# Ten Q-projection units row-tiled in pairs, with the filler matmuls placed ahead of them

## Chip, cores, metric

One core of one Trainium2 chip. The metric is the device time of one execution in microseconds (us), median of several runs.

## The reference

Input x has 2048 rows (tokens) and D = 576 columns. Both branches read the same layer norm of x, and the output is x plus both.

```python
xn = layernorm(x)
q, k, v = heads(xn @ wqkv)                 # 32 heads of 18
phi = lambda t: where(t > 0, t + 1, exp(t)) + 1e-6
kv  = einsum("bhsd,bhse->bhde", phi(k), v);  z = phi(k).sum(tokens)
A   = (phi(q) @ kv) / (phi(q) . z + 1e-6) @ wo
B   = (gelu(xn @ w_gate) * (xn @ w_up)) @ w_down      # 576 -> 4608 -> 576
return x + A + B
```

## The kernel before

Everything is written in one fixed order per engine. In the profiles PE is TensorE and SP is SyncE. PSUM is one tensor of eight banks, and the code names the bank of each product. The Q projection is made in 20 units (4 token chunks of 512, 5 head chunks of 126 or 72 columns). A unit contracts 576 = 4 x 128 + 64 rows, so its fifth matmul uses half of the array. Each unit's result then passes phi on ScalarE (ACT), VectorE (DVE) and, for two of three units, POOL; every third is finished on VectorE by a two-input add. Between the units stand other matmuls, the "filler".

```python
def phi_tiles():
    e = awork.tile([P, D], F32, name="phi_e", tag="phi_e", bufs=3)
    a = awork.tile([P, D], F32, name="phi_a", tag="phi_a", bufs=2)

def q_unit(i):
    ...
    for kt in range(KT):                                   # 5 matmuls on the full array
        nc.tensor.matmul(ps, lhsT=wqkv_sb[:, kt, q0:q0 + rows], rhs=xnT[:, kt, cs], ...)
    e, a = phi_tiles()
    if i % 3 != 2:
        nc.scalar.activation(out=e, in_=ps, func=ACT.Relu, scale=-1.0)
        nc.vector.tensor_scalar(out=a, in0=ps, ...)        # reads the bank too
        nc.scalar.activation(out=e, in_=e, func=ACT.Exp, scale=-1.0)
        nc.gpsimd.tensor_tensor(out=pqT[...], in0=e, in1=a, op=ALU.add)
    else:
        nc.scalar.activation(out=e, in_=ps, func=ACT.Exp)
        nc.vector.tensor_scalar(out=a, in0=ps, ...)
        nc.vector.scalar_tensor_tensor(out=pqT[...], in0=e, in1=a, ...)   # two SBUF inputs

for i in range(2, NSC * NCH):                              # cut: copies, early Gram, z
    q_unit(i)
    if 5 <= i < 13:  ...two g_accumulate(n, G_B)           # 4 Gram matmuls per unit
    if 13 <= i < 13 + NCH:  den_mm(0, i - 13, q_banks.next())
    if i == 17:  kv_stage()

class _Unit:                       # gate/up: gate and up share the array, 64 rows each
    def p1(self):                  # lower half adds into bank 0, upper half into bank 1
        for kt in (4, 0, 1, 2, 3):
            self.mm(0, LO, kt, kt == 4, False); last = self.mm(1, HI, kt, kt == 4, False)
        self.turn = nc.sync.nop()  # waits for `last`
    def p2(self):                  # the halves change banks; the first waits for turn
        for kt in range(4):
            self.mm(1, LO, kt, ...); self.mm(0, HI, kt, ...)
# a gate/up block: load, p1(u0), load, p1(u1), p2(u0), gelu, p2(u1), gelu
```

## Time and profile before

| | before |
|---|---|
| time, median of the first 3 runs | 532.59 us (532.07 to 533.60) |
| profiled span | 530.5 us |
| PE busy | 522.6 us |
| first Q matmul to first gate/up matmul | 45.06 to 77.59, 32.53 us |

All later intervals start at the first Q matmul, because the start of the kernel scatters by up to 0.45 us from trace to trace (the first Q matmul is between 45.06 and 45.51).

### The profile page before, as it was taken

What the parts mean: (1) busy time and instruction counts of PE and PEld (TensorE: products, weight loads), DVE (VectorE), ACT (ScalarE), POOL (GpSimd) and SP (SyncE); (2) the same over time, 40 slices, a digit from 0 to 9 for tenths busy, and PEclk for the clock granted to TensorE, in tenths of its full rate; (3) what the DMA queues carried; (4) which work ended last, traced back from release to release, by engine and by line L of the source; (5) the groups of instructions that cost most, each with busy time, mean ns of one, the idle gap of its engine ahead of it and who ended that gap; (6) DMA issues with size and microseconds to landing.
All of it is one profiled execution on the core that took longest, in us unless ns stands there. A gap on an engine that the chain in (4) does not pass through costs nothing.

```text
span 530.5 us, 10752 instructions
## 1 busy us (share of the span) xinstructions
PE 522.6 (99%) x4532; PEld 314.3 (59%) x4532; DVE 248.7 (47%) x408; ACT 152.5 (29%) x288; POOL 70.3 (13%) x83
## 2 busy tenths in 40 slices
PE   7999999999999999999999999999999999999997
PEld 5887666444467754444477744444677544445775
DVE  7885666783338613333368233333485143333101
ACT  6887783323330003323200022323100132322000
POOL 4666542110002100000012000000021000000000
PEclk9999999999999999999999999999999999999999
DMA  8910006898510025555400055555100345540000
GB/s 283 248 30 1 1 2 184 261 270 267 143 39 12 23 78 153 148 150 157 135 12 12 12 153 162 146 157 153 49 22 13 94 143 158 155 135 1 12 12 22
DMA packets 98810, 55.85 MB, mean 105 GB/s; under 512 B 5322, under 2 KB 98378, under 8 KB 98762
## 3 DMA queue, kind: packets, MB, share of 16 engines
q1 hardware_dynamic: 98762, 55.17, 36.2%
q8 instruction: 35, 0.57, 0.4%
q14 instruction: 13, 0.11, 0.1%
HBM read 52.79 MB, written 2.36 MB: 104 GB/s over the span
## 4 chain that ended last, share of the span: by engine, by line
PE 95%; SPq 2%; DVE 1%; ACT 1%; issue 0%; DMA 0%
PE ps_all L505 51%; PE ps_all L576 27%; PE ps_all L310 4%; PE ps_all L581 4%; PE ps_all L280 4%; PE ps_all L238 3%; PE ps_all L227 1%; SPq L166 1%; PE ps_all L370 1%; SPq L168 0%; SPq L169 0%; DMA x_sb<-in_A_x_dram 0%; ACT xnT L230 0%; DVE xn L217 0%; PE ps_all L358 0%
## 5 line engine op out<-in xcount | busy, mean ns | idle before, releaser
L505 PE MATMUL ps_all<-xnT,wg 64*128 64x512 bf16 x1152 | 274.1, 377 | 0.0
L505 PE MATMUL ps_all<-xnT,wu 64*128 64x512 bf16 x1152 | 272.6, 377 | 0.9 <-SPq L514 0.3
L549 DVE TENSOR_TENSOR hT<-ps_all,gl 128x512 bf16<-128x512 f32 x144 | 99.6, 692 | 168.9 <-ACT gl L548 168.7
L548 ACT ACTIVATE gl<-ps_all 128x512 f32<-128x512 f32 x144 | 86.0, 597 | 316.7 <-PE ps_all L505 294.9
L505 PEld LDWEIGHTS <-wu 64*128 64x128 bf16 x1152 | 106.9, 94 | 70.9 <-SPq L514 8.7
L505 PEld LDWEIGHTS <-wg 64*128 64x128 bf16 x1152 | 107.0, 94 | 66.7 <-issue 0.3
L576 PE MATMUL ps_all<-wd_sb,hT 128*128 128x288 bf16 x1152 | 146.6, 286 | 0.0
L576 PEld LDWEIGHTS <-hT 128*128 128x128 bf16 x1152 | 112.2, 98 | 31.5 <-issue 1.9
L384 DVE RECIPROCAL den_sb<-den_sb 126x128 f32<-126x128 f32 (+1 forms) x80 | 68.3, 911 | 0.5
L385 POOL TENSOR_TENSOR pqT<-pqT,den_sb 126x512 bf16<-126x512 bf16 (+3 forms) x25 | 24.1, 965 | 301.5 <-DVE den_sb L384 298.2
L584 DVE TENSOR_TENSOR res<-ps_all,x_sb 128x288 bf16<-128x288 f32 x32 | 14.6, 458 | 88.3 <-PE ps_all L581 88.3
L505 PE MATMUL ps_all<-xnT,wr 64*128 64x512 bf16 x288 | 55.9, 377 | 0.0
L581 PE MATMUL ps_all<-m_sb,pqT 126*128 126x288 bf16 (+1 forms) x160 | 24.9, 286 | 0.0
L505 PEld LDWEIGHTS <-wr 64*128 64x128 bf16 x288 | 14.6, 94 | 17.4 <-issue 1.1
L310 PE MATMUL ps_all<-xnT,wqkv_sb 128*126 128x512 bf16 (+1 forms) x100 | 24.4, 380 | 0.0
L265 POOL TENSOR_TENSOR hT<-phi_e,phi_a 128x576 bf16<-128x576 f32 x16 | 22.5, 1404 | 8.9 <-ACT phi_e L264 4.9
L280 PE MATMUL ps_all<-hT,xn 128*128 128x288 bf16 (+3 forms) x192 | 23.6, 266 | 0.0
L238 PE MATMUL ps_all<-wqkv_sb,xnT 128*128 128x288 bf16 x160 | 22.4, 286 | 0.8 <-DVE xnT L230 0.6
L280 PEld LDWEIGHTS <-xn 128*128 128x128 bf16 (+1 forms) x192 | 18.2, 101 | 4.5
L320 POOL TENSOR_TENSOR pqT<-phi_e,phi_a 126x512 bf16<-126x512 f32 (+1 forms) x14 | 17.7, 1268 | 15.5 <-DVE phi_a L318 11.8
L581 PEld LDWEIGHTS <-pqT 126*128 126x128 bf16 (+1 forms) x160 | 15.5, 97 | 4.1
L238 PEld LDWEIGHTS <-xnT 128*128 128x128 bf16 x160 | 15.0, 98 | 4.5 <-DVE xnT L230 0.8
(58 smaller groups left out, 200.6 us busy)
## 6 DMA issues: line engine op xcount, KB each, us to landing
wg<-in_B_w_gate_dram SPq DMA_DIRECT2D x72, 256.0 KB, 2.9
wu<-in_B_w_up_dram SPq DMA_DIRECT2D x72, 256.0 KB, 3.4
wd_sb<-in_B_w_down_dram SPq DMA_DIRECT2D x12, 432.0 KB, 4.5
wr<-in_B_w_gate_dram SPq DMA_DIRECT2D x72, 32.0 KB, 2.7
wr<-in_B_w_up_dram SPq DMA_DIRECT2D x72, 32.0 KB, 3.1
out_dram<-res SPq DMA_DIRECT2D x15, 144.0 KB, 1.8
x_sb<-in_A_x_dram SPq DMA_DIRECT2D x3, 576.0 KB, 6.6
wqkv_sb<-in_A_wqkv_dram SPq DMA_DIRECT2D x2, 576.0 KB, 9.2
```

The costliest lines, as they stand in the source:

```text
L238: nc.tensor.matmul(ps_all[:, k_bank(n, hf), :HALF], lhsT=xnT[:, kt, n * P:(n + 1) * P], rhs=wqkv_sb[:, kt, D + hf * HALF:D + (hf + 1) * HALF],
L265: nc.gpsimd.tensor_tensor(out=pk[:, n, :], in0=e[:], in1=a[:], op=ALU.add)
L280: nc.tensor.matmul(ps_all[:m, b, col:col + w], lhsT=xn[:, n, j0:j0 + m], rhs=pk[:, n, d0:d0 + w], start=(n == 0 and col == 0), stop=(n == ...
L310: nc.tensor.matmul(ps, lhsT=wqkv_sb[:, kt, q0:q0 + rows], rhs=xnT[:, kt, cs], start=(kt == 0), stop=(kt == KT - 1),)
L320: nc.gpsimd.tensor_tensor(out=pqT[:rows, c, cs], in0=e, in1=a, op=ALU.add)
L384: nc.vector.reciprocal(out=d[:, h:h + P], in_=d[:, h:h + P])
L385: nc.gpsimd.tensor_tensor(out=pqT[:rows, c, cols], in0=pqT[:rows, c, cols], in1=d, op=ALU.mult)
L505: return nc.tensor.matmul(self.outs[i], lhsT=self.lhs(i, rows, kt), rhs=self.rhs(i, rows, kt), start=start, stop=stop, skip_group_check=True,)
L548: nc.scalar.activation(out=gl[:], in_=ps_all[:, b[0], :], func=ACT.Gelu_apprx_tanh)
L549: nc.vector.tensor_tensor(out=hT[:, GUB * k + i, :], in0=ps_all[:, b[1], :], in1=gl[:], op=ALU.mult)
L576: nc.tensor.matmul(acc, lhsT=hT[:, f, j * P:(j + 1) * P], rhs=wd_sb[:, f, hs], start=(f == 0), stop=False,)
L581: nc.tensor.matmul(acc, lhsT=pqT[:rows, c, ts_], rhs=m_sb[:rows, c, hs], start=False, stop=(c == NCH - 1),)
```

## The change

Two Q units of the second half share the array as two row tiles of 64 rows: 9 slots of two half matmuls in place of 10 matmuls. All filler is placed ahead, so that the ten units run without a switch between the array's two modes, next to gate/up, which is row-tiled already. Gate/up's ring of banks now starts at bank 1, and the ring of the later m_stage is shifted too. Core of the diff:

```diff
+    wq_lo = apool.tile([P, D], BF16, name="wq_lo")        # last 64 rows of Wq for the upper half
+        if which == 0:
+            nc.sync.dma_start(wq_lo[HP:P, :], A_wqkv[512:576, c])
+    banks = _Ring([1, 2, 3, 4, 5, 6, 7, 0])
-    for i in range(2, NSC * NCH):
+    for i in range(2, 2 * NCH):
...
+        if i >= 4:
+            for n in G_B_AT[i]:
+                g_accumulate(n, G_B)
+    for c in range(NCH):
+        den_mm(0, c, q_banks.next())
+    kv_stage()
+    q_banks = _Ring([7, 0, 1, 2, 3, 4, 5, 6])
+    for k, items in enumerate([[(2, 0), (2, 1)], [(2, 2), (2, 3)], [(2, 4), (3, 4)], [(3, 0), (3, 1)], [(3, 2), (3, 3)], None]):
+        if items:
+            u = q_pair(items)
+            u.p1()
+        if prev:
+            prev[1].p2()
+            for i, (sc, c) in enumerate(prev[0]):
+                q_phi(2 * k + i, sc, c, prev[1].outs[i])
+        prev = (items, u)
```

I number the paired units by the index that q_phi gets, 2 to 11; 2, 5, 8 and 11 are finished on VectorE. Unit 11 has bank 0.

More of the change, by code (lines that the diff above doesn't have):

```diff
@@ L283, in g_accumulate @@
                 )
+    G_B_AT = {4: (), 5: (0, 1), 6: (2, 3, 4), 7: (5, 6, 7), 8: (8, 9, 10, 11), 9: (12, 13, 14, 15)}
     vcopy, acopy = nc.vector.tensor_copy, nc.scalar.copy
@@ L298, with __init__, mm, p1 @@
     q_next = [0]
+    LO, HI = slice(0, HP), slice(HP, P)
+    SYNC = mybir.DependencyInfo(mybir.DependencyClass.Sync, mybir.DependencyReason.DATA)
+    banks = _Ring([1, 2, 3, 4, 5, 6, 7, 0])
+    class _Unit:
+        def __init__(self, outs, lhs, rhs):
+            self.outs, self.lhs, self.rhs = outs, lhs, rhs
+        def mm(self, i, rows, kt, start, stop):
+            return nc.tensor.matmul(
+                self.outs[i], lhsT=self.lhs(i, rows, kt), rhs=self.rhs(i, rows, kt),
+                start=start, stop=stop, skip_group_check=True,
+            )
+        def p1(self):
+            for kt in (4, 0, 1, 2, 3):
+                self.mm(0, LO, kt, kt == 4, False)
+                last = self.mm(1, HI, kt, kt == 4, False)
+            self.turn = nc.sync.nop()
+            tc.add_manual_dep(self.turn.ins, last.ins.name, SYNC, reason="the row tiles take turns on a bank")
+        def p2(self):
+            for kt in range(4):
+                m = self.mm(1, LO, kt, False, kt == 3)
+                if kt == 0:
+                    tc.add_manual_dep(m.ins, self.turn.ins.name, SYNC, reason="the bank's other row tile has written")
+                self.mm(0, HI, kt, False, kt == 3)
     q_banks = _Ring([7])
@@ L306, in q_unit @@
         q0 = DH * HOFF[c]
-        cs = slice(sc * SC, (sc + 1) * SC)
         ps = ps_all[:rows, q_banks.next(), :]
@@ L310, in q_unit, with q_pair, lhs, q_phi @@
             nc.tensor.matmul(
-                ps, lhsT=wqkv_sb[:, kt, q0:q0 + rows], rhs=xnT[:, kt, cs],
+                ps, lhsT=wqkv_sb[:, kt, q0:q0 + rows], rhs=xnT[:, kt, sc * SC:(sc + 1) * SC],
                 start=(kt == 0), stop=(kt == KT - 1),
             )
+        q_phi(i, sc, c, ps)
+    def q_pair(items):
+        rows = DH * HCH[items[0][1]]
+        b = [q_banks.next(), q_banks.next()]
+        outs = [ps_all[:rows, b_, :] for b_ in b]
+        def lhs(i, r, kt):
+            q0 = DH * HOFF[items[i][1]]
+            if kt == 4 and r.start:
+                return wq_lo[r, q0:q0 + rows]
+            return wqkv_sb[r, kt, q0:q0 + rows]
+        return _Unit(outs, lhs, lambda i, r, kt: xnT[r, kt, items[i][0] * SC:(items[i][0] + 1) * SC])
+    def q_phi(i, sc, c, ps):
+        rows = DH * HCH[c]
+        cs = slice(sc * SC, (sc + 1) * SC)
         e, a = phi_tiles()
@@ L464 @@
             g_copy(kt, pieces, part, copy)
-        if i == 10:
+        if i >= 4:
+            for n in G_B_AT[i]:
+                g_accumulate(n, G_B)
+        if i == 8:
             z_stage()
-        if 5 <= i < 13:
-            for n in (2 * (i - 5), 2 * (i - 5) + 1):
-                g_accumulate(n, G_B)
-        if 13 <= i < 13 + NCH:
-            den_mm(0, i - 13, q_banks.next())
-        if i == 17:
-            kv_stage()
+    for kt, pieces, part, copy in G_COPIES[14]:
+        g_copy(kt, pieces, part, copy)
+    for c in range(NCH):
+        den_mm(0, c, q_banks.next())
+    kv_stage()
+    q_banks = _Ring([7, 0, 1, 2, 3, 4, 5, 6])
+    prev = None
+    for k, items in enumerate([[(2, 0), (2, 1)], [(2, 2), (2, 3)], [(2, 4), (3, 4)], [(3, 0), (3, 1)], [(3, 2), (3, 3)], None]):
[7 more added lines that the diff above has]
+        prev = (items, u)
     den_jobs = [(0, c, q, 2) for c in range(NCH) for q in range(2)]
@@ L488, in load_wd_slice @@
             wd_loaded[0] += WDS
-    LO, HI = slice(0, HP), slice(HP, P)
-    SYNC = mybir.DependencyInfo(mybir.DependencyClass.Sync, mybir.DependencyReason.DATA)
-    banks = _Ring(list(range(8)))
-    class _Unit:
-        def __init__(self, outs, lhs, rhs):
-            self.outs, self.lhs, self.rhs = outs, lhs, rhs
-        def mm(self, i, rows, kt, start, stop):
-            return nc.tensor.matmul(
-                self.outs[i], lhsT=self.lhs(i, rows, kt), rhs=self.rhs(i, rows, kt),
-                start=start, stop=stop, skip_group_check=True,
-            )
-        def p1(self):
-            for kt in (4, 0, 1, 2, 3):
-                self.mm(0, LO, kt, kt == 4, False)
-                last = self.mm(1, HI, kt, kt == 4, False)
-            self.turn = nc.sync.nop()
-            tc.add_manual_dep(self.turn.ins, last.ins.name, SYNC, reason="the row tiles take turns on a bank")
-        def p2(self):
-            for kt in range(4):
-                m = self.mm(1, LO, kt, False, kt == 3)
-                if kt == 0:
-                    tc.add_manual_dep(m.ins, self.turn.ins.name, SYNC, reason="the bank's other row tile has written")
-                self.mm(0, HI, kt, False, kt == 3)
     def gu_pair(sc, k):
@@ L549, in gu_pair @@
             nc.vector.tensor_tensor(out=hT[:, GUB * k + i, :], in0=ps_all[:, b[1], :], in1=gl[:], op=ALU.mult)
-    m_banks = _Ring(list(range(2, 8)))
+    m_banks = _Ring([3, 4, 5, 6, 7, 0])
     def m_stage(chunks):
```

## The prediction

> **What bounds the kernel now.** I read the page first, then the chain of work that ended last, then the busy table by stage, then the timeline of the one stage that the change touches. The chain's sum by engine:
>
> ```profile
> PE 95%; SPq 2%; DVE 1%; ACT 1%; issue 0%; DMA 0%
> ```
>
> So a microsecond counts only if TensorE (PE) gives it up or is made to wait. The stages, cut at the points where the chain changes its kind of matmul (columns: stretch, length, busy time of PE, weight loads, VectorE, ScalarE, POOL, then clock, DMA share, GB/s):
>
> ```profile
> 0.00:45.00 45.00, 41.63 (x395) 34.21 (x396) 35.98 (x99) 36.12 (x85) 25.75 (x42) 1.00 0.59 165
> 45.00:77.60 32.60, 32.60 (x212) 22.03 (x211) 20.27 (x36) 24.53 (x47) 17.99 (x14) 1.00 0.00 1
> 77.60:149.00 71.40, 71.33 (x654) 34.74 (x654) 42.95 (x60) 24.51 (x42) 9.21 (x12) 1.00 0.74 216
> ```
>
> The second line is the Q stage: PE busy in all 32.60 us, no transfers, full clock. The third is the first quarter of gate/up, in row tiles already. Inside the Q stage:
>
> ```profile
> 65.63 0.60 ACT L323 ACTIVATE phi_e<-ps_all 126x512 f32<-126x512 f32 x1 [0.52 <-PE ps_all L310]
> 66.33 0.69 DVE L324 TENSOR_SCALAR phi_a<-ps_all 126x512 f32<-126x512 f32 x1 [0.43 <-ACT phi_e L323]
> 67.06 0.69 DVE L325 SCALAR_TENSOR_TENSOR pqT<-phi_e,phi_a 126x512 bf16<-126x512 f32 x1
> 67.26 0.60 ACT L317 ACTIVATE phi_e<-ps_all 126x512 f32<-126x512 f32 x1 [1.03 <-PE ps_all L310]
> 67.49 1.24 PE L310 MATMUL ps_all<-xnT,wqkv_sb 128*126 128x512 bf16 x5
> 67.96 0.69 DVE L318 TENSOR_SCALAR phi_a<-ps_all 126x512 f32<-126x512 f32 x1 [0.21 <-ACT phi_e L317]
> 68.57 0.38 PE L370 MATMUL ps_all<-pqT,zrep 126*126 126x512 bf16 x1
> 68.79 1.24 PE L310 MATMUL ps_all<-xnT,wqkv_sb 128*72 128x512 bf16 x5
> 68.80 1.27 POOL L320 TENSOR_TENSOR pqT<-phi_e,phi_a 126x512 bf16<-126x512 f32 x1 [2.21 <-DVE phi_a L318]
> ...
> 75.31 2.35 PE L310 MATMUL ps_all<-xnT,wqkv_sb 128*126 128x512 bf16 x10
> ...
> 77.59 0.39 PE L505 MATMUL ps_all<-xnT,wr 64*128 64x512 bf16 x2
> ...
> 78.12 1.27 DVE L318 TENSOR_SCALAR phi_a<-ps_all 126x512 f32<-126x512 f32 x2
> ```
>
> PE starts are what to read, since a matmul's 0.38 us overlaps the next. 67.49 to 68.57 is a unit of five matmuls: 1.08 us, 0.2166 each. 68.57 to 68.79 is one denominator matmul, 0.22. No gap between them. The other engines wait for PE here (0.5 to 2.2 us in brackets), because filler stands between Q units: a unit comes every 1.30 us with a denominator, every 1.57 us (65.92 to 67.49) with four Gram matmuls.
>
> **What the Trainium skill says.** "TensorEngine Tiling (Array Packing)", Key Properties: different tiles run in parallel, and changing the mode drains the array. The trace agrees: the last full matmul begins at 75.31 + 9 x 0.2166 = 77.26, the first row-tiled one at 77.59, 0.33 later where 0.217 is normal, so a switch costs 0.12. The change makes that switch earlier, not more often. Same page, PSUM Bottleneck: tiling does not speed up what empties PSUM. That is my main worry; the brackets above show that there is slack now, but only thanks to the filler. "TensorE: Matmul & The Clock Gate", Weight-path perf modes: fast weight load wants 128 weights; Q has 126 or 72. The trace shows 136 ns for a 126-column load against 98 for one of 128, still hidden, and in the kv product 25 matmuls of 126 columns run in 1.32 us (73.99 to 75.31), 53 ns each with their loads. Two such loads fit in 0.2166 us even one after the other, so I expect no limit from weights. "PSUM — Partial Sum Buffer", PSUM bank collisions raise a hardware error: engines may not touch a bank at once. In the trace VectorE indeed starts 0.03 to 0.1 us after ScalarE has ended on the same bank, so the two reads of a Q unit are in series.
>
> **The change part by part.** D is 576 = 4 x 128 + 64. A full unit spends five matmuls, the fifth half empty. A pair of units in row tiles needs 18 half matmuls, two at a time: 9 slots instead of 10. Removed: 50 full matmuls, 10 x 1.083 = 10.83 us. Added: 90 halves, 45 slots x 0.2166 = 9.75 us (the gate/up row-tiled pairs run at that rate: 512 of them in 55.46 us, 0.2166 per two). **Gain on PE: 1.08 us.** One more 64 x 576 load, early and in a stage with room: nothing. Handovers between row tiles: the waiting half comes at least a whole phase (0.87 us) after the half that it waits for, and the SyncE queue is empty then: nothing.
>
> Moved: Gram remainder, denominators and kv product keep their matmuls, so PE time is unchanged. Positions in the new order, from before's start of unit 4 (53.60): units 4 to 9 (6 x 1.083), 32 Gram matmuls (3.92) and the z product (0.26) end at 64.27, five denominators at 65.35, kv at 66.67, switch to 66.79, five pairs at 76.53 (before 77.59). Three tight places on the way. The first denominator needs the masked z: unit 8 leaves PE at 60.97, its VectorE work ends 2.31 later as for unit 8 before, 63.28, the mask by 64.1: 0.2 spare. The first pair needs bank 7, which denominator 1 held; ScalarE's evictions at 0.67 each free it at 66.5: 0.3 spare. kv needs the last Gram copy near 65.2 to 65.4: spare. I allow 0.1 us for these together.
>
> **The price: PSUM banks at the start of gate/up.** With the filler gone, a unit comes every 1.95 / 2 = 0.975 us, 2.92 per three. Of each three units one is finished on VectorE alone and two on POOL, and the buffer phi_a has two copies. So the third unit's first VectorE read waits until POOL has released the copy two units back. One turn: first read 0.72 to its dependent add, add 0.59 to the next independent operation (spacing of the two in 78.12, 1.27 long), read 0.69, hop to POOL 0.15, add on POOL 1.27, hop back about 0.05: **3.47 us per three units against 2.92 on PE**. Starting from pair 1's end (PE at 69.82, ScalarE at 70.08 to 70.68, VectorE at 70.78): unit index 3 is read at 72.09, its copy is free at 74.25; index 5 is read from 74.25, index 8 from 77.72, index 11 from 81.19 to 81.88. Index 11 lies in the second bank of the last pair, number 0. The gate/up units take banks 1-2, 3-4, 5-6, 7-0; the fourth begins two and a half phases later: 76.53 + 2 x 1.083 + 2 x 0.866 + 1.083 = 81.51. So PE waits there until about 81.9: **0.4 us given back.** Bank pair 5-6 (index 9, read by about 79.8) is needed at 80.43, free. Later, the activation table load and the first gelus have 3 us of room before bank 1 is wanted again.
>
> Sum: 532.59 - 1.08 + 0.10 + 0.40 = **532.0 us**, 0.1% faster.
>
> **Rivals.**
> 1. No give-back: 531.5. For it: before, VectorE sat idle 2.2 us before its first gate/up product, and ScalarE's table load could start at 79.09, 1.5 after gate/up began; eight banks buffer much. Against: in the new order the last two units arrive together exactly at the switch, and that slack was made by filler.
> 2. Eviction is the full bound: if POOL slows (it shares work with busier VectorE; one dependent add took 0.78 instead of 0.69 in this stage) each three units cost 0.2 more, index 11 is late by another 0.6, and index 9 delays banks 5-6 too: 532.6 to 533, no gain or a small loss.
> 3. Row tiles with 126 columns don't run two at a time, or their loads don't hide: 90 x 0.2166 = 19.5 instead of 9.75, a loss near 8.7 us: 541. Against: gate/up does it with 64 rows and 128 columns at the full rate, and the slower load is 136 ns. I give it 1%.
> 4. The weights for down, placed where Q's weights and phi buffers lay, wait longer and hold up the SyncE queue. Their first issue was at 84.2 us, the tail of phi now ends near 82.6, and the next handover behind it is needed near 86: hidden.
>
> **Range and chances.** The unknowns are the give-back (0 to 1.0 us) and the timing itself: three runs of before span 532.07 to 533.60, so a median of three can be off by 0.4. Range 531.2 to 532.9. Two per cent is 10.7 us, ten times the whole gain; only rival 3 comes near it on the slow side: same 0.98, slower 0.01, faster 0.01.
>
> **What would show it.** Right: row-tiled Q starts 0.2166 us apart per two; gate/up starts near 76.5 us; a wait of 0.2 to 0.7 us by a gate/up matmul about 5 us later, put down to VectorE reading a Q bank; VectorE's or POOL's phi work in a turn of about 3.5 us per three units, with waits on each other where before they waited for PE; from the first down stage on all starts shifted by one constant of about -0.6 us. Wrong: no such wait (rival 1); waits already between the pairs or at the denominators, so that gate/up starts after 77; or starts in row tiles wider than 0.22 us.

## The result, and the profile after

| | before | after |
|---|---|---|
| median of 6 runs | 532.33 us (531.39 to 533.60) | 532.93 us (532.30 to 533.37) |
| ratio, 95% interval | | 1.0008 (0.9993 to 1.0023) |
| first Q matmul to gate/up | 32.53 us | 31.46 us |
| fourth to fifth gate/up unit | 2.81 us | 3.63 us |
| first Q matmul to first down matmul | 104.55 us | 104.45 us |

Executions in which one die ran at a lower clock are left out of the means. A ratio is the mean time of one kernel's fast runs over that of the other's of the same rounds, so it is not quite the ratio of the medians quoted. By the clock nothing happened. The trace shows two opposite things of about 1 us each. Busy table by stage, the changed kernel (columns as in the prediction):

```profile
45.36:76.82 31.46, 31.46 (x251) 21.48 (x249) 18.28 (x34) 21.80 (x42) 14.14 (x11) 1.00 0.01 1
76.82:149.50 72.68, 71.67 (x655) 32.30 (x652) 46.22 (x64) 26.81 (x47) 11.71 (x14) 1.00 0.74 213
```

The Q stage is 1.07 us shorter and still has no gap. The gate/up stage holds the loss: 72.68 us long with 71.67 busy. Up to the first down matmul it takes 72.99 us (76.82 to 149.81), where the kernel before takes 72.02 (77.59 to 149.61). Its place, in PE's timeline of the changed kernel (start, length, line, operation; in brackets the idle time before and who ended it):

```profile
76.82 0.38 PE L321 MATMUL ps_all<-xnT,wr 64*128 64x512 bf16 x2
...
80.70 0.38 PE L321 MATMUL ps_all<-xnT,wr 64*128 64x512 bf16 x2
...
81.78 0.38 PE L321 MATMUL ps_all<-xnT,wr 64*128 64x512 bf16 x1
82.81 0.37 PE L321 MATMUL ps_all<-xnT,wr 64*128 64x512 bf16 x1 [0.65 <-DVE phi_a L382]
...
85.41 0.57 PE L321 MATMUL ps_all<-xnT,wr 64*128 64x512 bf16 x2
```

Each gate/up unit begins with a matmul on wr, two at a time. The fourth began alone at 81.78: its partner, which writes bank 0, came 1.03 later. The bracket says 0.65 because idle time is counted from the modelled end of the matmul before. The cost is best read from the next unit: 81.78 to 85.41 is 3.63, where the kernel before has 2.81 (82.56 to 85.37), so 0.82 us:

```profile
82.56 0.54 PE L505 MATMUL ps_all<-xnT,wr 64*128 64x512 bf16 x2
...
85.37 0.54 PE L505 MATMUL ps_all<-xnT,wr 64*128 64x512 bf16 x2
```

The other 0.21, one slot, is not lost yet, because the lower half has done one matmul ahead; but the halves now run one slot apart (85.41 is marked 0.57 long, two starts of 0.38), and at the end of the quarter the later one counts. VectorE's timeline says why the read of unit 11 (the last L382) is so late:

```profile
71.02 0.69 DVE L382 TENSOR_SCALAR phi_a<-ps_all 126x512 f32<-126x512 f32 x1 [3.21 <-ACT phi_e L381]
71.75 0.69 DVE L383 SCALAR_TENSOR_TENSOR pqT<-phi_e,phi_a 126x512 bf16<-126x512 f32 x1
72.36 1.29 DVE L376 TENSOR_SCALAR phi_a<-ps_all 126x512 f32<-126x512 f32 x2
74.48 0.69 DVE L382 TENSOR_SCALAR phi_a<-ps_all 126x512 f32<-126x512 f32 x1 [0.83 <-POOL pqT L378]
75.20 1.02 DVE L383 SCALAR_TENSOR_TENSOR pqT<-phi_e,phi_a 126x512 bf16<-126x512 f32 x1
76.15 1.27 DVE L376 TENSOR_SCALAR phi_a<-ps_all 72x512 f32<-72x512 f32 x2
78.27 0.69 DVE L382 TENSOR_SCALAR phi_a<-ps_all 126x512 f32<-126x512 f32 x1 [0.85 <-POOL pqT L378]
...
82.06 0.69 DVE L382 TENSOR_SCALAR phi_a<-ps_all 126x512 f32<-126x512 f32 x1 [0.84 <-POOL pqT L378]
```

From one L382 to the next, three units, it takes 3.46 us in the first turn, then 3.79 and 3.79. Every turn ends in a wait of 0.8 for POOL; what the later turns have in addition is an add (L383) that takes 1.02 where the first took 0.69. POOL's timeline of the changed kernel:

```profile
73.18 2.49 POOL L378 TENSOR_TENSOR pqT<-phi_e,phi_a 126x512 bf16<-126x512 f32 x2 [6.54 <-DVE phi_a L376]
76.97 2.50 POOL L378 TENSOR_TENSOR pqT<-phi_e,phi_a 72x512 bf16<-72x512 f32 x2 [1.29 <-ACT phi_e L377]
```

POOL's two adds end at 75.67 and 79.47; VectorE's adds end at 76.22 and 80.02, each 0.55 later. The two-input add seems to stand still until POOL has ended. That is what the Trainium skill says in "SBUF — State Buffer", Who interferes with whom: "A DVE instruction with two SBUF inputs contends with a GpSimd instruction that reads SBUF", and the one that comes second blocks. I had not looked there. VectorE's two largest waits from 65 us on, up to 82 us before and 86 us after (total, times, longest):

```profile
DVE phi_a L324 <- ACT phi_e L323: 2.6, 3, 1.1
DVE phi_a L318 <- ACT phi_e L317: 2.5, 4, 0.8
```

```profile
DVE phi_a L382 <- ACT phi_e L381: 3.2, 1, 3.2
DVE phi_a L382 <- POOL pqT L378: 2.5, 3, 0.8
```

Before, VectorE waited for fresh results from ScalarE and in turn from PE; after, for a buffer to come free.

### The profile page after: what moved, and what is told of

Its sections match the earlier page's. It is cut to its first block, busy times and chain, and to the rows that moved or that the text cites. A ratio compares the mean times of both kernels' runs of the same rounds, so it can differ in the third digit from the quotient of the medians.

```text
span 530.6 us, 10832 instructions
## 1 busy us (share of the span) xinstructions
PE 522.2 (98%) x4572; PEld 311.8 (59%) x4572; DVE 249.9 (47%) x409; ACT 151.7 (29%) x287; POOL 69.0 (13%) x82
## 4 chain that ended last, share of the span: by engine, by line
PE 93%; SPq 2%; ACT 1%; POOL 1%; DVE 1%; issue 1%; POOLq 0%; ACTq 0%
PE ps_all L321 51%; PE ps_all L614 27%; PE ps_all L619 4%; PE ps_all L285 4%; PE ps_all L243 3%; PE ps_all L349 2%; PE ps_all L232 1%; SPq L171 1%; PE ps_all L428 1%; POOL pqT L378 1%; PE ps_all L137 1%; SPq L173 0%; SPq L174 0%; ACT phi_e L377 0%; ACT phi_e L375 0%
## 5 line engine op out<-in xcount | busy, mean ns | idle before, releaser
L378 POOL TENSOR_TENSOR pqT<-phi_e,phi_a 126x512 bf16<-126x512 f32 (+1 forms) x13 | 16.4, 1268 | 18.3 <-DVE phi_a L376 11.4
L263 DVE TENSOR_SCALAR phi_a<-ps_all 128x288 f32<-128x288 f32 x32 | 13.3, 448 | 1.5 <-ACT phi_e L262 1.4
```

What stands on the lines that cost most here:

```text
L378: nc.gpsimd.tensor_tensor(out=pqT[:rows, c, cs], in0=e, in1=a, op=ALU.add)
```

## The experiments

Theory: row tiling gives PE 1.07 us, and 0.82 us or a little more go back at bank 0, because phi_a has only two copies and POOL locks out VectorE's add. Rivals: the order alone makes the wait; the engines' own rate is the bound and copies don't matter; phi_e is what holds the chain. In all of them the "wait" is the fourth-to-fifth distance less 2.81; the delay of the partner itself can be a slot (0.2 us) more, and is what counts by the first down matmul.

**e1_copies**, more copies:

```diff
-tag="phi_e", bufs=3   ...   tag="phi_a", bufs=2
+tag="phi_e", bufs=4   ...   tag="phi_a", bufs=3
```

> The changed kernel with one more copy of each phi buffer (phi_a 3 instead of 2, phi_e 4 instead of 3). Theory (the last Q unit's read waits for POOL to release a copy of phi_a, so bank 0 comes free late): VectorE no longer waits for POOL between Q units, bank 0 is read by about 4.3 us after gate/up begins, and the 0.82 us wait of the fourth gate/up unit is gone; first to fifth gate/up unit 7.8 us instead of 8.6; total about 0.8 us below the changed kernel, 531.5 to 532.1. Rival (the rate of VectorE, ScalarE and POOL themselves is the bound, copies do not matter): the wait stays at 0.5 us or more and only moves to another releaser.

531.88 us (531.12 to 532.95) against 533.05 of before in its rounds, ratio 0.9981 (0.9969 to 0.9994). VectorE's last read, and the fourth and fifth gate/up unit, in the timeline of this run:

```profile
80.44 0.69 DVE L382 TENSOR_SCALAR phi_a<-ps_all 126x512 f32<-126x512 f32 x1
...
81.54 0.38 PE L321 MATMUL ps_all<-xnT,wr 64*128 64x512 bf16 x2
...
84.35 0.38 PE L321 MATMUL ps_all<-xnT,wr 64*128 64x512 bf16 x2
```

The read ends at 81.13, before the bank is wanted at 81.54; both halves start together and the distance is 2.81: no wait. The rate rival falls. The chain still slows down inside (adds of 1.5 and 1.6 us beside POOL), but it fits.

**e8_a_only** and **e9_e_only** split that edit: bufs=3 for phi_a alone, bufs=4 for phi_e alone.

> The changed kernel with a third copy of phi_a alone. Theory (the chain that sets bank 0's release runs through phi_a's two copies): most of the 0.82 us wait goes; ScalarE still waits for POOL over phi_e, so a wait of 0 to 0.4 us stays. Rival (phi_e, where ScalarE waits 0.4 and 0.8 us, is what holds the chain): the wait stays near 0.8 us.

> The changed kernel with a fourth copy of phi_e alone. Theory: the wait of the fourth gate/up unit stays at 0.7 to 0.9 us, VectorE still waits three times 0.8 us for POOL. Rival: the wait falls below 0.4 us.

The wait was 0.05 us with the third phi_a (81.50 to 84.36) and 0.84 with the fourth phi_e (81.57 to 85.22). With phi_a alone, though, the fourth unit is marked 0.63 long, so its partner was still 0.25 late:

```profile
81.50 0.63 PE L321 MATMUL ps_all<-xnT,wr 64*128 64x512 bf16 x2
```

So phi_a is most of it, 1.03 down to 0.25; only both copies together, as in e1_copies, leave nothing. By the clock the first does not show: 532.32 us, but from 531.14 to 534.09, ratio 1.0002 (0.9981 to 1.0024); e9_e_only took 533.43, ratio 1.0019. That scatter had to be explained too, see below.

**e2_order_only**, the new order with the ten units on the full array:

```diff
-            u = q_pair(items); u.p1() ...  prev[1].p2()
+        for kt in range(KT):
+            nc.tensor.matmul(ps, lhsT=wqkv_sb[:, kt, q0:q0 + rows], rhs=xnT[:, kt, ...], ...)
+        q_phi(k + 2, sc, c, ps)
```

> The changed kernel's order (Gram remainder, denominators, kv first), but its last ten Q units on the full array, one after the other, 50 matmuls. Theory: the phi chain needs 3.79 us per three units, PE now gives three in 3.25, but the first unit is there 2 us earlier since no second phase is waited for: no wait at bank 0, gate/up begins 1.07 us later than in the changed kernel (measured from the first Q matmul), total that of the kernel before within 0.3 us. Rival (the order alone, by taking the filler away, makes the wait): a wait of 0.3 us or more at the fourth gate/up unit and a total 0.3 to 1 us above the kernel before.

First Q matmul to gate/up 32.51 us, as before (32.53); fourth to fifth unit 82.60 to 85.40, no wait. The trace decides here; the clock says 533.34 us with runs from 530.70 to 534.36, ratio 1.0004. So the order is neutral by itself: all of the 1.07 us is the row tiles', and the wait appears only together with them. But the slow turn is there without row tiles:

```profile
75.96 0.69 DVE L382 TENSOR_SCALAR phi_a<-ps_all 126x512 f32<-126x512 f32 x1 [0.84 <-POOL pqT L378]
76.69 1.02 DVE L383 SCALAR_TENSOR_TENSOR pqT<-phi_e,phi_a 126x512 bf16<-126x512 f32 x1
...
79.75 0.69 DVE L382 TENSOR_SCALAR phi_a<-ps_all 126x512 f32<-126x512 f32 x1 [0.85 <-POOL pqT L378]
```

Its turns take 3.47, 3.79 and 3.79 us, as in the changed kernel; it is the order that brings VectorE's add and POOL's together. What the row tiles do is to start that chain 2.07 us later (the first L382 at 25.66 after the first Q matmul, against 23.59 here) and to ask for the bank 1.07 us earlier. Here the last read ends at 80.44, 2.16 before the bank is wanted at 82.60.

**e4_all_vector**, no POOL in the paired units:

```diff
-        if i % 3 != 2:
+        if i % 3 != 2 and not dve:        # dve=True for the pairs
```

> The changed kernel with all ten paired Q units finished on VectorE, none on POOL. Asks why VectorE's two-input add took 1.02 us instead of 0.69 in the paired stage. If POOL's adds at the same time cause it: all ten adds take 0.69, a unit costs VectorE 1.3, the last read ends about 12.4 us after the first begins and the fourth gate/up unit waits about 1.5 us; total 0.7 us above the changed kernel. If it is something else (the row tiles, PSUM traffic): the adds take 1.02, a unit 1.65, the wait is above 4 us, total 3.5 us above.

All ten adds took 0.69 us and a unit 1.33. VectorE's last unit:

```profile
82.80 0.68 DVE L382 TENSOR_SCALAR phi_a<-ps_all 126x512 f32<-126x512 f32 x1
83.52 0.69 DVE L383 SCALAR_TENSOR_TENSOR pqT<-phi_e,phi_a 126x512 bf16<-126x512 f32 x1
```

The same add, in the same row-tiled stage, is slow only while POOL adds. The expected 1.5 us of waits came as 0.30, 0.29 and 1.12 before the third, fourth and fifth unit, 1.71 together; 533.89 us, ratio 1.0015 (1.0002 to 1.0028).

**e7_before_copies**, the kernel before with e1's edit, as a control.

> Control: the kernel before with one more copy of each phi buffer. Theory: there VectorE waits for PE and ScalarE, never for POOL's release, so nothing moves: gate/up begins at the same time from the first Q matmul, total within 0.3 us of before. If it gains 0.5 us or more, the copies help by another way than the theory says and the first run proves less.

32.53 us to gate/up, no waits between the units there; 532.52 us, ratio 0.9990 (0.9977 to 1.0003). The copies do nothing where the filler keeps phi ahead.

**e5_after_again**, the changed kernel once more:

> The changed kernel once more, on the same chip as its variants: total within 0.3% of before, the wait of the fourth gate/up unit again 0.82 us by the trace (0.7 to 0.9).

532.56 us (531.18 to 534.19), ratio 1.0004; the wait again 0.83 (81.54 to 85.18).

**Where the scatter comes from.** With a change worth tenths, runs that spread over 1 to 3.7 us can't settle it. In every trace some gate/up units are late without any Q work near. Two cases, first of the kernel before, then of e1_copies (SPq: a DMA being issued by SyncE):

```profile
91.22 1.30 SPq L169 DMA_DIRECT2D wr<-in_B_w_up_dram  x1
...
92.64 0.39 PE L505 MATMUL ps_all<-xnT,wu 64*128 64x512 bf16 x1
```

```profile
101.42 1.67 SPq L173 DMA_DIRECT2D wu<-in_B_w_up_dram  x1
...
103.76 0.39 PE L321 MATMUL ps_all<-xnT,wu 64*128 64x512 bf16 x1 [0.50 <-SPq L330]
```

An issue that mostly takes 0.4 to 0.5 us now and then takes 1.1 to 2.0, and the handover between the row tiles (L330, L514 before) is a nop behind it in the same queue. The excess distances of all gate/up units in the profile of before sum to 2.74 us, nine late units; three of them, of 0.3 us each at the starts of quarters, follow issues of 0.39 to 0.58, so not every late unit has a long issue before it. So I moved the handover, in three kernels:

```diff
-            self.turn = nc.sync.nop()
+            self.turn = eng.nop()
-            u.p1()
+            u.p1(nc.scalar if blk >= 2 else nc.sync)
```

> The version with the extra phi copies, and from the third gate/up block on the handover between row tiles put on ScalarE's queue in place of SyncE's, where it stands behind weight loads. Theory (the other waits in gate/up, 1.8 us beside the 0.3 us at each quarter's start in the trace of e1_copies, come from a load whose issue takes 1.1 to 1.9 us instead of 0.5 and holds up the handover behind it): these waits go, total 1 to 2 us below e1_copies, near 530.3, and the scatter of the runs falls below that of before. Rival (they come from the weights themselves, or the handover now waits for gelu): total as e1_copies or above.

> The kernel before with the handover on ScalarE's queue: the same gain, 1 to 2 us below before, near 531; with it the comparison of before and after is made without that noise.

> The changed kernel with the handover on ScalarE's queue. Theory: without the noise the change is worth 1.07 - 1.03 us (a wait of 0.82 and one lone half matmul of 0.22), so this lies within 0.3 us of e12_before_turn, and e11_copies_turn 0.7 to 1.1 us below both. Rival (the change costs elsewhere too): 0.5 us or more above e12_before_turn.

| handover on ScalarE | median (range) | Q to gate/up | wait | Q to first down |
|---|---|---|---|---|
| e12_before_turn | 529.59 (529.55 to 529.89) | 32.53 | 0 | 104.33 |
| e13_after_turn | 529.38 (529.29 to 529.80) | 31.46 | 0.84 | 104.11 |
| e11_copies_turn | 528.55 (528.22 to 528.92) | 31.46 | 0 | 103.09 |

Before in the same rounds: 532.34; the ratios are 0.9950 (0.9937 to 0.9962), 0.9947 (0.9934 to 0.9959) and 0.9931 (0.9917 to 0.9944). The handover was worth 2.75 us to the kernel before, as much as its late units summed to, and more than I had expected; no unit is late any more, not even at the quarters' starts, which I had counted as fixed. The long issues themselves are still there (1.78 us at 234.76 in the trace of e12_before_turn) and no unit is late behind them, so it was the handover's place in the queue and not weights that came late. With the spread at 0.3 to 0.7 us, the copies show by the clock, 0.8 us (529.38 to 528.55). The change alone comes out 0.2 us ahead of before (529.59 to 529.38), but with five runs each and ranges that overlap this is not shown by the clock; both profiled spans are 527.9. The last column closes the account: e13_after_turn is 1.02 us behind e11_copies_turn, which is the partner's whole delay at bank 0 (1.04 in this trace), and 0.22 ahead of e12_before_turn, by one trace of each.

**e10_seven_pairs** and **e14_seven_turn**: e1_copies with seven pairs, the filler moved ahead of unit 5 (narrow unit 9 taken early); the second with the z product's copies one unit earlier and the handover on ScalarE.

```diff
-    for i in range(2, 2 * NCH):
+    for i in (2, 3, 4, 9):
-    ...enumerate([[(2, 0), (2, 1)], ...
+    ...enumerate([[(1, 0), (1, 1)], [(1, 2), (1, 3)], [(2, 0), (2, 1)], ...
```

> The version with the extra copies (e1_copies), the filler moved further ahead (Gram remainder, denominators and kv straight after unit 4 and the narrow unit 9) and seven pairs instead of five. Theory: two more pairs save 2 x 0.2166 = 0.43 us of PE; from the first Q matmul to gate/up 31.0 us instead of 31.46. The reads of e1_copies ran at 3.2 us per three units against 2.92 on PE, so four more units make the last read 0.4 us later, which its slack of 0.6 us just holds: no wait, total about 0.4 us under e1_copies. Rival: VectorE and POOL fall further behind (the add that is locked out by POOL takes up to 1.6 us), a wait of 0.3 us or more comes back and the gain is gone.

A miss: 31.34 us to gate/up in place of 31.0, since z waited 0.27 us for its copies; the wait at the fourth gate/up unit was back at 0.30 (81.38 to 84.49), as its rival had it, and several handovers were late in its trace. 532.49 us, ratio 1.0000 (0.9987 to 1.0014).

> e10_seven_pairs with its two losses mended: the copies that the z product waits for (0.27 us in the trace of e10_seven_pairs) are made one unit earlier, and the handover is on ScalarE's queue as in e11_copies_turn. Theory: from the first Q matmul to gate/up 31.03 us (31.46 - 2 x 0.2166), no wait at the fourth gate/up unit, total 0.43 us below e11_copies_turn, near 528.1. Rival (the phi work of four more units overruns): a wait of 0.3 us or more at a gate/up unit and a total at or above 528.5.

Half a miss: 31.02 us to gate/up as expected, but VectorE's last read ended at 81.51 while the fourth unit had begun at 81.06, and the wait was again 0.30, which neither of the two edits had addressed. The unit is marked 0.88 long, so the partner was 0.50 late, more than the 0.43 gained: 103.15 us to the first down matmul, where e11_copies_turn has 103.09. 528.43 us (528.25 to 528.92), ratio 0.9922 (0.9908 to 0.9936): not distinguishable from e11_copies_turn. Two more pairs bring phi to its limit again.

## Why the prediction was right, and where it was off

- **No measurable change, 532.0 us.** Right in kind. The measured median, 532.93, lies 0.03 above the range's printed end (532.9). The total tests little: every give-back from 0 to 1 us stays within the range and the scatter, so the size of the sum was not confirmed by it. In the quiet pair the change is worth 0.2 us (not clear of noise) where 0.6 was predicted, and the shift by the first down stage is 0.1 to 0.2.
- **Gain on PE 1.08 us, filler neutral, switch only moved.** Right: 32.53 to 31.46 is 1.07, and e2_order_only gives 0.02 to the order.
- **Three tight places, 0.1 us.** None of them waited: the Q stage is busy throughout.
- **126-column weights no limit.** Right: 1.94 us per pair (68.40 to 70.34), although their loads take 133 ns against 94 for gate/up's.
- **The price at bank 0, 0.4 us.** The mechanism was right to the bank, the unit and the buffer (e1_copies, e8_a_only, e9_e_only). The size was off. The term that failed is "add 0.59 to the next independent operation". It held in the first turn (predicted 3.47, measured 3.46), when POOL was idle; in the next two the add's start to the next read's start was 0.95, and a turn 3.79. Two turns of 0.32 more are 0.64 us. The read of unit 11 ended 0.97 after the fourth gate/up unit began (82.75 against 81.78), where 0.37 was predicted (81.88 against 81.51); the hop to PE adds 0.06. So the give-back was 1.02 by the first down matmul in place of 0.4. The sign that was named, a wait of 0.2 to 0.7, came as 0.65 in the profile's bracket but as 1.03 between starts. Rival 2 of the prediction drew a slowdown from one add of 0.78 us, 0.2 per turn and 0.6 for index 11, and the size came true; but it has POOL slow down, and in the trace POOL's adds keep their length (2.49 for two) while VectorE's is held up. It should have been the main line, because the filler's going makes POOL and VectorE meet in each turn after the first; e2_order_only shows this.
- **The timing, 0.4 us.** The scatter was taken as given. It had a cause, the handover behind loads, that was visible in the chain of before as 2% SPq. "Handovers between row tiles: nothing" was right for the Q pairs only.
- **Rival 4, down's weights hold up SyncE.** Not seen: the first of these loads was issued at 84.27 in the changed kernel, 84.20 before, and no unit waited behind it.

Left open: why an issue sometimes takes three times as long; no run here tells. Also, from gate/up's start to the first down matmul e11_copies_turn takes 71.63 us and e12_before_turn 71.80; with the 1.07 gained and the 1.02 given back, this 0.17 makes up the 0.22 by which the change wins. In e12's trace, as in before's, the two halves run a little apart from the second unit on (78.78 is marked 0.54 long); that this is the cause was not tested.

## What to carry to other kernels

Filler that looks like an interruption may be what keeps the emptying of PSUM ahead; before moving it, add up one turn of the eviction chain with the buffers that it reuses and with the engines that will now run at the same time. A gain on the bounding engine of one microsecond reaches the end only if the buffer that the next stage wants is free by then, and one more copy of a small tile (2.3 KB per partition) can be the whole difference. And when the effect is smaller than the scatter, look for the scatter's cause first: here it was worth more than ten times what the change brought.

## What the Trainium skill lacked or had wrong

- "SBUF — State Buffer", Who interferes with whom: had it right, and the prediction should have used it. The runs add the size: VectorE's 512-column two-input add took 0.69 us alone, 1.02 beside POOL's add, up to 1.82 (e8_a_only) where it began 1.27 before the end of POOL's, and in both cases ended 0.55 after POOL's.
- "TensorEngine Tiling (Array Packing)", Gotcha 1: it asks software to synchronise row tiles on a bank, but does not say what that costs. Here the handover through a queue that also issues loads cost 2.75 us of 532; through ScalarE's queue no unit was late.
- Same page, Key Properties: the drain at a mode switch has no figure there; the trace of before shows 0.12 us beyond the normal distance.
- "TensorE: Matmul & The Clock Gate", Weight-path perf modes: nothing there on row tiles with fewer than 128 columns; the runs show 126-column loads of 133 ns, two per slot, hidden behind 0.2166 us slots.
- No page that I found tells that a DMA's issue sometimes holds its queue several times as long as usual: 0.51 us by the median for the 32 KB loads of the kernel before, up to 1.99 (e2_order_only) in these traces.
